# One pipeline of 33 steps for the later two thirds, its first weights fetched earlier, and the sums' steps spread wider

## The chip, the cores and the metric

The kernel runs on one core of one Trainium2 chip. The metric is device time in microseconds, the median of three runs: 2182.09 before (2181.76 to 2184.82). One core has five instruction streams, each executed in order: TensorE (PE, with its weight loads shown apart as PEld), VectorE (DVE), ScalarE (ACT), GpSimd (POOL) and SyncE (SP). In this kernel SP issues every DMA, so a DMA that waits on SP holds up all those written behind it. Engines and DMAs meet by semaphores only.

## The reference, cut to what matters

```python
q_p, k_p = phi(q_s), phi(k_s)                 # random-feature attention, 4 x 8 heads, 576 tokens, 128 features
x = (q_p @ (k_p.T @ v)) / (q_p @ z + 1e-6)    # -> x: 2304 tokens x 512
g = x @ w_gate                                # first layer, 512 -> 1536 -> 512
x = (silu(g) * (x @ w_val)) @ w_out
P = exp(x @ w_gate2 - max)                    # 2304 x 8, then 8 rounds of row and column scaling
for e in range(8):                            # second layer: every expert sees every token
    out += P[:, e:e + 1] * (np.maximum(x @ w1[e], 0) @ w2[e])     # 512 -> 1024 -> 512
```

All of it is in float32 to float32's accuracy. The kernel gets that from TensorE by splitting every operand into a high part (one copy by ACT that rounds) and a low part (a subtraction), and by three matmuls for each product: high x high, high x low, low x high.

## The kernel before

**The first layer** (`moe1`) has 6 groups of 256 hidden features, and for each group 6 blocks of 384 tokens. A block is two hidden units (`hunit`, 24 matmuls each) with the output unit of the block before between them (`ounit`, 24 matmuls, L753 to L755): 72 matmuls. Behind each hidden unit ACT runs the silu (L730), DVE multiplies (L731), ACT rounds the product to its high part (L734) and DVE makes the low part (L735); the output unit reads both. Between matmuls two generators are pumped, one step at a time: background tasks that prepare weights (`m1_task`, L155 on), and `sums` (L295), which prepares the combined forms of the second layer's down weights for later. `sums` has 32 rounds. A round loads one tile of weights (`raw2`), forms four combinations on POOL (L306 to L309), waits some steps, rounds two tiles on ACT (L322), subtracts on DVE (L324), and writes the results to DRAM (L317). A block of `moe1` has 14 places at which `sums` may take a step: five in each hidden unit, four in the output unit. So where an ACT instruction of `sums` stands against the silu of a hidden unit is set by counting steps.

**The second layer** multiplies by a scheme of seven products in place of eight 2x2 block products. For that the 768 tokens of a third need seven combined forms of x, each with high and low part: `b11`, `b21`, `b22`, `t1` to `t4`. `make_xops` builds them. A **quad** is the seven products for one group of hidden features.

The first third of the tokens (`moe2`) makes and uses the weights' forms and writes them to DRAM. For each of 16 groups m it runs `quad(m, 0)`, the output of group m-1 (`yunits`), `quad(m, 1)`. The outputs `yunits(15)` run alone at the end; `make_xops` for the second third is pumped beside them, and then the last weight forms are written.

The later two thirds (`thirds`) read finished weight forms from DRAM. For each third t there are 17 steps s. In a step, slots j = 0 to 13 each issue one product of the quads of group s (`quad_product`, 6 matmuls, L1237 to L1239) and one product of the outputs of group s-1 (`second_product`, 6 matmuls into half of a PSUM pair, L1321 to L1323); step 0 has only the former and step 16 only the latter. Behind every second output product DVE adds the pair to an accumulator (L1329). In step 16 DVE also combines the seven accumulators into four (L1332). Each quad is followed by gates (L1250, which need the token's gate weights `p`), ACT roundings (L1253), four subtractions on POOL (L1260), and low parts on DVE or POOL (L1257). Weights come as units of 512 KB into a ring of 11; `load` (L1189) asks for the next one or two at odd slots. `load_p` (L1203) fetches the gates' weights. The third's results are transposed by TensorE (`out_tile`, L1342), copied by ACT (L1344) and stored: those of the second third in step 0 of the last one, those of the last after everything.

Before the change the first units and the first gates' weights are asked for when the first third is over:

```python
1347  load(len(units))
1348  load_p(1, 0)
```

## Time and profile before

| what | value |
|---|---|
| median of three runs | 2182.09 us |
| the profiled execution, its own time | 2183.46 us |
| its span, first to last instruction | 2181.7 us |
| PE busy | 2106.2 us (97%) |
| DVE, POOL, ACT busy | 1340.2, 1014.1, 831.5 us (61, 46, 38%) |
| mean granted clock of TensorE | 0.986 of full speed |

What is not busy on PE is little, so the table alone says nothing of a change. The idle time lies in a few places: by the timeline, 22 us in the first layer, 19.5 us around 1189 to 1227 us where the first third ends, 6 us around 1670 to 1708 us where the second third ends, and some 6 us behind 2165 us. PE is also marked busy while it runs at half clock, which it does in some stretches behind such holes; the stage tables therefore carry the granted clock.

### The profile page before, as it was taken

To read this page: it belongs to the slowest core of one execution; us is meant where nothing else is said; L and a number is where in the kernel's file an instruction comes from. 1 tells how busy PE (TensorE), PEld (TensorE's weight loads), DVE (VectorE), ACT (ScalarE), POOL (GpSimd) and SP (SyncE) were. 2 spreads that over 40 slices of the span, in tenths; PEclk is the share of its full clock that TensorE was granted. 3 is DMA by queue.
4 is the path that set the end of the run, shared out by engine and by line. 5 is a ranking of instruction groups with operands and counts; after the bars stand their busy time and mean duration, and the time that the engine had idled before them with its cause. 6 is when DMAs were issued, how large, how long until landed. Compare 5 with 4: busy or idle time off the path is not lost.

```text
span 2181.7 us, 32894 instructions
## 1 busy us (share of the span) xinstructions
PE 2106.2 (97%) x12029; PEld 2025.7 (93%) x12029; DVE 1340.2 (61%) x2334; ACT 831.5 (38%) x1855; POOL 1014.1 (46%) x1034
## 2 busy tenths in 40 slices
PE   8999998998999999999998799999999999999998
PEld 7999998998999889989997799999998999999997
DVE  6886566666655654444445466666667666666666
ACT  6775333233244354334432332333233523332332
POOL 6663656565453444554551344344433443444442
PEclk9999999999999999999999899999999999999998
DMA  4332554554323567666674787777877777878773
GB/s 132 107 93 93 178 183 155 171 169 154 115 78 142 204 215 262 249 229 243 253 255 176 253 259 257 258 253 248 295 259 234 259 259 256 260 257 259 253 255 116
DMA packets 255153, 455.29 MB, mean 209 GB/s; under 512 B 42800, under 2 KB 137616, under 8 KB 250896
## 3 DMA queue, kind: packets, MB, share of 16 engines
q1 hardware_dynamic: 254992, 453.19, 62.3%
q8 instruction: 95, 1.56, 0.3%
q14 instruction: 66, 0.54, 0.1%
HBM read 327.76 MB, written 125.35 MB: 208 GB/s over the span
## 4 chain that ended last, share of the span: by engine, by line
PE 80%; DVE 6%; DMA 4%; POOL 4%; issue 3%; ACT 2%; SPq 1%; POOLq 0%; DVEq 0%; ACTq 0%
PE bank L1028 12%; PE pair L1321 7%; PE pair L1323 7%; PE pair L1322 7%; PE bank L1237 7%; PE bank L1239 7%; PE bank L1238 7%; PE bank L969 4%; PE bank L971 3%; PE bank L970 3%; DMA w2raw<-in_moe_w_dram 2%; PE bank L722 2%; PE bank L723 2%; PE bank L724 2%; PE bank L561 1%
## 5 line engine op out<-in xcount | busy, mean ns | idle before, releaser
L1237 PE MATMUL bank<-xh,ar 128*128 128x384 f32 x896 | 302.3, 337 | 20.3 <-DVE mt L1275 11.2
L1239 PE MATMUL bank<-xh,ar 128*128 128x384 f32 x896 | 301.1, 336 | 0.0
L1238 PE MATMUL bank<-xl,ar 128*128 128x384 f32 x896 | 301.1, 336 | 0.0
L1329 DVE TENSOR_TENSOR sums<-pair,sums 128x768 f32<-128x768 f32 x210 | 199.7, 951 | 48.3 <-PE pair L1323 48.0
L722 PE MATMUL bank<-xh,ar 128*128 128x384 f32 x576 | 192.8, 335 | 0.0
L724 PE MATMUL bank<-xh,ar 128*128 128x384 f32 x576 | 192.5, 334 | 0.0
L723 PE MATMUL bank<-xl,ar 128*128 128x384 f32 x576 | 192.4, 334 | 0.0
L1237 PEld LDWEIGHTS bank<-xh,ar 128*128 128x128 f32 x896 | 169.6, 189 | 22.3 <-DVE mt L1275 11.8
L1321 PE MATMUL pair<-xh,ar 128*128 128x384 f32 x538 | 180.6, 336 | 1.7 <-DVE sums L1329 1.7
L1322 PE MATMUL pair<-xl,ar 128*128 128x384 f32 x538 | 179.8, 334 | 0.0
L1323 PE MATMUL pair<-xh,ar 128*128 128x384 f32 x538 | 179.8, 334 | 0.0
L1238 PEld LDWEIGHTS bank<-xl,ar 128*128 128x128 f32 x896 | 169.5, 189 | 0.0
L1239 PEld LDWEIGHTS bank<-xh,ar 128*128 128x128 f32 x896 | 169.5, 189 | 0.0
L969 PE MATMUL bank<-xh,ar 128*128 128x384 f32 x448 | 151.7, 339 | 6.1 <-DVE st L1003 5.8
L237 POOL TENSOR_TENSOR ar<-w1raw,ar 128x512 fp32r<-128x512 f32 x64 | 65.3, 1030 | 193.4 <-ACT ar L235 92.6
L971 PE MATMUL bank<-xh,ar 128*128 128x384 f32 x448 | 150.8, 337 | 0.1
L970 PE MATMUL bank<-xl,ar 128*128 128x384 f32 x448 | 150.4, 336 | 0.0
L1044 DVE SCALAR_TENSOR_TENSOR ac<-bank,mt,ac 128x512 f32<-128x512 f32 x84 | 63.0, 750 | 127.8 <-PE bank L1028 126.0
L753 PE MATMUL bank<-ar,ar 128*128 128x384 f32 x288 | 101.7, 353 | 21.5 <-ACT ar L734 21.5
L1028 PE MATMUL bank<-ar,xh 128*128 128x512 f32 x402 | 115.2, 393 | 0.0
L324 DVE TENSOR_TENSOR ar<-w2raw,ar 128x512 fp32r<-128x512 f32 x64 | 58.9, 927 | 84.5 <-ACT ar L322 63.1
L722 PEld LDWEIGHTS bank<-xh,ar 128*128 128x128 f32 x576 | 108.1, 188 | 0.1
(270 smaller groups left out, 5662.3 us busy)
## 6 DMA issues: line engine op xcount, KB each, us to landing
ar<-w1forms SPq DMA_DIRECT2D x224, 512.0 KB, 4.9
ar<-w2forms SPq DMA_DIRECT2D x224, 512.0 KB, 4.5
w2forms<-ar SPq DMA_DIRECT2D x376, 128.0 KB, 3.5
w1forms<-ar SPq DMA_DIRECT2D x32, 1280.0 KB, 7.6
w2raw<-in_moe_w_dram SPq DMA_DIRECT2D x64, 512.0 KB, 3.9
w1raw<-in_moe_w_dram SPq DMA_DIRECT2D x32, 512.0 KB, 4.3
w1forms<-ar SPq DMA_DIRECT2D x32, 512.0 KB, 8.1
m1raw<-in_moe_w_gate_dram SPq DMA_DIRECT2D x12, 512.0 KB, 4.1
```

The lines of the kernel that those rows point to most:

```text
L722: nc.tensor.matmul(t, hi[:, c, fs], self.xh[:, c, cs], start=(c == 0), stop=False)
L723: nc.tensor.matmul(t, hi[:, c, fs], self.xl[:, c, cs], start=False, stop=False)
L724: nc.tensor.matmul(t, lo[:, c, fs], self.xh[:, c, cs], start=False, stop=(c == KC - 1))
L969: nc.tensor.matmul(g, ah[:, c, :], bh[:, c, :], start=(first and c == 0), stop=False, skip_group_check=not first)
L971: nc.tensor.matmul(g, al[:, c, :], bh[:, c, :], start=False, stop=(c == 1), skip_group_check=not first)
L1028: nc.tensor.matmul(y, a, w[:, fi % 2, ds], start=(first and x == 0 and k == 0 and fi == fis[0]), stop=(last and x == 1 and fi == fis[-1]))
L1237: nc.tensor.matmul(g, w[:, 0, d], bh[:, d, :], start=bool(first and d == 0), stop=False, skip_group_check=not first)
L1238: nc.tensor.matmul(g, w[:, 0, d], bl[:, d, :], start=False, stop=False, skip_group_check=not first)
L1239: nc.tensor.matmul(g, w[:, 1, d], bh[:, d, :], start=False, stop=(d == 1), skip_group_check=not first)
L1321: nc.tensor.matmul(pair[:, b, :], w[:, k, 0, ds], h, start=(k == 0), stop=False)
L1322: nc.tensor.matmul(pair[:, b, :], w[:, k, 0, ds], l, start=False, stop=False)
L1323: nc.tensor.matmul(pair[:, b, :], w[:, k, 1, ds], h, start=False, stop=(k == 1))
```

## The change

Five edits:

1. `sums` takes three more steps in each round: five in place of four between the combinations and the first rounding, one before the next load and one behind it.
2. The ring of units, the first six loads and the list of what to load become methods. `load_units(6)` stands ahead of the last quad of the first third, and five more together with the first gates' weights ahead of `yunits(15)`. The remaining writes of weight forms stand there too. So on SP these loads come ahead of the six stores of the first third's results.
3. `make_forms` takes the place of `make_xops(..., True)`. Forms come in the order in which the quad uses them, and seven of their eleven subtractions of 128x768 move from DVE to POOL.
4. The later two thirds are one loop of 33 steps: step 16 runs the first quads of the last third beside the last outputs of the second. The forms of the last third are made from slot 8 of step 15 to slot 1 of step 16. The second third's results are transposed in slots 0 to 5 of step 17, through one PSUM bank.
5. The last step takes its outputs in another order (`LAST2`), with the sums of accumulators spread over it and one of them, (5, 7), on POOL, in both thirds. The last six tiles go through six different PSUM banks and six buffers, copied by ACT and DVE in turn.

```diff
+    LAST2 = (1, 3, 5, 6, 7, 2, 4)
@@ sums
-            for _ in range(4):
+            for _ in range(5):
                 yield
@@
                     for _ in range(3):
                         yield
+            yield
             if i + 1 < len(order):
                 t = load(i + 1)
+            yield
             for c in range(one, 2):
                 write(c)
@@ new
+    def make_forms(self, pf, qf):
...
+        p0, p1, q0, q1 = pf[:, 0:2, :], pf[:, 2:4, :], qf[:, 0:2, :], qf[:, 2:4, :]
+
+        def form(n, src, eng):
+            h, l = [self.xslot(x, *self.XS[n]) for x in range(2)]
+            nc.scalar.copy(h, src)
+            eng.tensor_tensor(l, src, f(h), op=ALU.subtract)
+
+        def sub(dst, a, b):
+            g.tensor_tensor(dst, a, b, op=ALU.subtract)
+
+        form("b11", p0, g)
+        yield
+        sub(p0, q0, p0)
+        yield
+        form("t1", p0, v)
+        sub(q0, q1, q0)
+        yield
+        sub(p0, q1, p0)
+        yield
+        form("t2", p0, v)
+        form("b21", p1, g)
+        yield
+        sub(p1, p1, p0)
+        form("t3", q0, v)
+        yield
+        form("b22", q1, g)
+        yield
+        form("t4", p1, v)
+        yield
@@ moe2
+            if m == NG2 - 1:
+                self.set_units()
+                self.load_units(6)
             hs = hs + drive(quad(m, 1), self.PACE['g2'], self.PACE['r01'] if m == 0 else self.PACE['rq'])
@@
-        xg = self.make_xops(*stage, True)
+        for i in range(2):
+            self.need(("w2", NG2 - 1, i))
+        self.set_weights()
+        self.load_units(5)
+        while self.writes:
+            self.writes.popleft()()
+        xg = self.make_forms(*stage)
         self.bg.appendleft(xg)
         drive(yunits(*pend))
         for _ in xg:
             pass
-        while self.writes:
-            self.writes.popleft()()
@@ thirds, second_product
             if m == NG2 - 1:
-                for d, a in {2: [(2, 1)], 5: [(3, 5)], 6: [(1, 6), (7, 1), (3, 1), (5, 7)], 4: [(4, 7)]}.get(n, ()):
-                    v.tensor_tensor(acc[d], acc[d], acc[a], op=ALU.add)
+                rest = [(7, 1), (4, 7), (5, 7)]
+                sums = {1: [(2, 1)], 5: [(3, 5)], 6: [(1, 6), (3, 1)]}
+                sums.setdefault(7 if step > m else 6, []).extend(rest)
+                for d, a in sums.get(n, ()):
+                    eng = nc.gpsimd if d == 5 else v
+                    eng.tensor_tensor(acc[d], acc[d], acc[a], op=ALU.add)
@@ thirds, the loop
+        for g in range(self.STEPS):
+            if g == NG2 - 1:
+                xg = self.make_forms(*stage)
+            for j in range(14):
+                if g < 2 * NG2:
+                    quad_product(g, j)
+                run_later()
+                if g == NG2 + 1 and j < 6:
+                    out_tile(1, j, self.banks[3 if self.nquad % 2 else 0], spare((6, 7)[j % 2]), nc.scalar)
+                if g:
+                    second_product(g - 1, j)
+                if 14 * g + j >= 14 * (NG2 - 1) + 8 and g <= NG2:
+                    next(xg, None)
+                if j % 2:
+                    self.load_units((g < 2 * NG2) + (g > 0))
+                if j == 11 and g % 2 == 0 and g < 2 * NG2 - 2:
+                    self.load_p(g // 2 + 1)
+                now[0] += 1
...
+        room = [spare(n) for n in (1, 6, 7)] + [x[:, 0:DM] for x in self.lasts]
+        banks = self.banks[0:4] + [self.pairs[1][:, i * 512:(i + 1) * 512] for i in range(2)]
         for i in range(6):
-            out_tile(2, i)
+            out_tile(2, i, banks[i], room[i], (nc.scalar, v)[i % 2])
```

What this does to the order of instructions, at three places. First ACT in the third group of the first layer, where `w2raw` is a tile of `sums` (its rounding is L322 before and L323 after), `mt <- bank` is a silu and `m1raw` and `cv` belong to the weight tasks. Before:

```order
L734 CAST ar_62<-mt_2394 128x384
L322 CAST ar_62<-w2raw_0_4029 128x512 x2
L730 ACTIVATE mt_2394<-bank_71 128x384
L734 CAST ar_62<-mt_2394 128x384
L199 CAST ar_61<-cv 128x512
L182 ACTIVATE m1raw_1_0_4056<-m1raw_1_0_4056 128x512
L322 CAST ar_62<-w2raw_1_4130 128x512
L730 ACTIVATE mt_2394<-bank_69 128x384
L734 CAST ar_62<-mt_2394 128x384
L322 CAST ar_62<-w2raw_1_4130 128x512
L730 ACTIVATE mt_2394<-bank_71 128x384
```

And after, further into the layer:

```order
L323 CAST ar_62<-w2raw_0_4591 128x512 x2
L733 ACTIVATE mt_2394<-bank_69 128x384
L737 CAST ar_62<-mt_2394 128x384
L733 ACTIVATE mt_2394<-bank_71 128x384
L737 CAST ar_62<-mt_2394 128x384
L200 CAST ar_61<-cv 128x512
L183 ACTIVATE m1raw_1_0_4672<-m1raw_1_0_4672 128x512
L323 CAST ar_62<-w2raw_1_4711 128x512 x2
L733 ACTIVATE mt_2394<-bank_69 128x384
L737 CAST ar_62<-mt_2394 128x384
L733 ACTIVATE mt_2394<-bank_71 128x384
L737 CAST ar_62<-mt_2394 128x384
```

The roundings of `sums` still stand ahead of silus, but a round comes every 15 steps in place of 12, with five steps between its combinations and its first rounding.

Second, SP where the first third ends: `w1forms` and `w2forms` are the weight forms in DRAM (a row `w2forms<-...` writes them, a row `ar<-...` loads a unit), `pweights` the gates' weights, `out_dram` the results. Before:

```order
L1382 DMA out_dram<-ac_6623 128x512 x2
L1382 DMA out_dram<-ac_6622 128x512 x4
L287 DMA w2forms<-w2a 128x256 x3
L287 DMA w2forms<-w2b 128x256 x3
L1199 DMA ar_61<-w1forms 128x2x512 x2
L1199 DMA ar_61<-w1forms 128x1024
L1199 DMA ar_61<-w1forms 128x2x512 x3
L1199 DMA ar_62<-w1forms 128x2x512 x2
L1196 DMA ar_62<-w2forms 128x1024
L1199 DMA ar_62<-w1forms 128x2x512
L1196 DMA ar_62<-w2forms 128x1024
L1205 DMA last_10643<-pweights 128x6x128
```

After:

```order
L1222 DMA ar_61<-w1forms 128x2x512 x2
L1222 DMA ar_61<-w1forms 128x1024
L1222 DMA ar_61<-w1forms 128x2x512 x3
L1232 DMA last_10531<-pweights 128x6x128
L1222 DMA ar_62<-w1forms 128x2x512 x2
L1219 DMA ar_62<-w2forms 128x1024
L1222 DMA ar_62<-w1forms 128x2x512
L1219 DMA ar_62<-w2forms 128x1024
L288 DMA w2forms<-w2a 128x256 x3
L288 DMA w2forms<-w2b 128x256 x3
L1438 DMA out_dram<-ac_6623 128x512 x2
L1438 DMA out_dram<-ac_6622 128x512 x4
```

All eleven loads and the gates' weights stand ahead of the six stores, and six loads and the gates' weights ahead of anything that the last outputs release.

Third, POOL where the second third ends, with `xl` the low parts and `st`, `mt`, `last`, `sums` the working tiles. Before (two quads of the last steps of the second third):

```order
L1260 TENSOR_TENSOR sums_10639<-sums_10639,sums_10641 128x384
L1257 TENSOR_TENSOR xl<-last_10645,xh 128x384 x2
L1260 TENSOR_TENSOR mt_2394<-mt_2394,last_10645 128x384
L1260 TENSOR_TENSOR mt_2394<-last_10645,mt_2394 128x384
L1260 TENSOR_TENSOR st_6625<-last_10645,mt_2394 128x384
L1260 TENSOR_TENSOR mt_2394<-mt_2394,st_6625 128x384
```

After, between the same two quads (L875 and L878 are `make_forms`):

```order
L1313 TENSOR_TENSOR sums_10654<-sums_10654,sums_10656 128x384
L875 TENSOR_TENSOR xl<-st_6625,xh 128x2x384
L878 TENSOR_TENSOR st_6625<-mt_2394,st_6625 128x768
L878 TENSOR_TENSOR mt_2394<-mt_2394 128x768
L878 TENSOR_TENSOR st_6625<-mt_2394,st_6625 128x768
L1310 TENSOR_TENSOR xl<-last_10533,xh 128x384
L875 TENSOR_TENSOR xl<-st_6625,xh 128x2x384
L1310 TENSOR_TENSOR xl<-last_10533,xh 128x384
L878 TENSOR_TENSOR st_6625<-st_6625 128x768
L1313 TENSOR_TENSOR mt_2394<-mt_2394,last_10533 128x384
L1313 TENSOR_TENSOR mt_2394<-last_10533,mt_2394 128x384
L1313 TENSOR_TENSOR st_6625<-last_10533,mt_2394 128x384
```

Seven wide subtractions of the forms (the seventh stands a row below) now stand among the narrow ones of the last quad of the second third.

## Rows read from the trace of the kernel before

**Rows 1.** The page: busy time of each engine, share of span, instructions.
```profile
PE 2106.2 (97%) x12029; PEld 2025.7 (93%) x12029; DVE 1340.2 (61%) x2334; ACT 831.5 (38%) x1855; POOL 1014.1 (46%) x1034
```

**Rows 2.** Windows, first layer's six groups: length, busy PE PEld DVE ACT POOL, clock.
```profile
178.10:255.56 77.46, 75.71 (x471) 74.71 (x470) 42.94 (x73) 34.17 (x71) 34.07 (x34) 1.00 0.44 140
255.56:340.90 85.34, 79.39 (x434) 77.85 (x433) 52.20 (x89) 27.83 (x55) 50.66 (x50) 0.96 0.54 172
340.90:426.14 85.24, 78.68 (x433) 76.90 (x433) 52.41 (x92) 26.60 (x51) 49.91 (x47) 0.96 0.53 170
426.14:510.89 84.75, 79.06 (x433) 77.41 (x433) 53.38 (x93) 26.34 (x52) 49.94 (x48) 0.96 0.52 168
510.89:589.02 78.13, 76.22 (x433) 74.69 (x433) 48.53 (x88) 23.77 (x46) 41.27 (x36) 1.00 0.42 136
589.02:673.00 83.98, 83.98 (x486) 82.87 (x486) 46.60 (x83) 32.58 (x68) 32.20 (x25) 1.00 0.22 80
```

**Rows 3.** Windows, two blocks of the fourth group.
```profile
466.70:479.18 12.48, 12.48 (x73) 12.48 (x73) 6.28 (x13) 4.14 (x8) 6.45 (x7) 1.00 0.55 171
491.66:510.89 19.23, 15.57 (x73) 15.16 (x73) 11.62 (x23) 4.81 (x10) 10.77 (x12) 0.82 0.51 170
```

**Rows 4.** Waits, 178 to 589: total us, times, longest.
```profile
ACT ar L322 <- POOL w2raw L308: 97.4, 22, 7.3
POOL w2raw L306 <- DMA w2raw<-in_moe_w_dram: 91.6, 25, 20.8
...
ACT ar L199 <- POOL cv L196: 34.7, 14, 4.0
...
ACT ar L322 <- DMA w2forms<-ar: 26.2, 9, 4.0
...
PE bank L753 <- ACT ar L734: 21.5, 11, 4.0
```

**Rows 5.** One combination of the sums (L308), and landing of their loads (L273).
```profile
L308 POOL TENSOR_TENSOR w2raw<-w2raw 128x256 f32<-128x256 f32 x32 | 26.0, 813 | 2.5
...
DMA to landing us min/median/max: 3.7/3.9/6.9
```

**Rows 6.** Windows: first seam, second seam, one full step, tail.
```profile
1188.90:1229.30 40.40, 20.71 (x91) 19.79 (x92) 12.48 (x20) 6.99 (x15) 8.70 (x8) 0.75 0.75 262
1668.78:1710.31 41.53, 35.13 (x199) 32.56 (x199) 39.35 (x50) 17.66 (x33) 12.00 (x11) 1.00 0.68 210
1710.31:1739.40 29.09, 29.09 (x169) 28.99 (x168) 16.25 (x24) 14.36 (x27) 15.37 (x16) 1.00 0.81 280
2166.00:2181.70 15.70, 6.17 (x24) 4.57 (x24) 4.46 (x5) 3.52 (x6) 0.00 (x0) 0.58 0.32 100
```

**Rows 7.** Timeline of PE, first seam: start, us, ... idle before and its releaser.
```profile
1196.71 0.66 PE L1237 MATMUL bank<-xh,ar 128*128 128x384 f32 x1 [7.84 <-DMA ar<-w1forms]
...
1216.74 0.69 PE L1237 MATMUL bank<-xh,ar 128*128 128x384 f32 x1 [10.80 <-DVE mt L1275]
```

**Rows 8.** Timeline in yunits(15): the first addition, and PE's fifth output.
```profile
1179.39 0.75 DVE L1044 SCALAR_TENSOR_TENSOR ac<-bank,mt,ac 128x512 f32<-128x512 f32 x1
...
1183.27 0.39 PE L1028 MATMUL bank<-ar,xh 128*128 128x512 f32 x1
```

**Rows 9.** Subtractions of 128x768 by engine: ns min/median/max.
```profile
L835 POOL TENSOR_TENSOR mt<-mt,mt x3: 2046/2150/2166, 626.0 to 632.3; 128x768 f32<-128x768 f32 x3
...
L832 DVE TENSOR_TENSOR xl<-st,xh x8: 946/949/959, 1173.8 to 1688.4; 128x768 fp32r<-128x768 f32 x8
L832 POOL TENSOR_TENSOR xl<-mt,xh x4: 1842/1848/1852, 640.0 to 664.9; 128x768 fp32r<-128x768 f32 x4
```

**Rows 10.** Low parts on DVE (two SBUF inputs): ns min/median/max.
```profile
L1257 DVE TENSOR_TENSOR ar<-last,ar x25: 549/559/1406, 1251.3 to 2143.9; 128x384 fp32r<-128x384 f32 x25
```

**Rows 11.** Timeline of the tail: PE, ACT, SP.
```profile
2169.55 0.69 PE L1342 MATMUL pair<-ident,sums 128*128 128x128 f32 x2 [3.55 <-DVE sums L1329]
...
2177.99 0.59 ACT L1344 COPY sums<-pair 128x512 f32<-128x512 f32 x1 [1.25 <-PE pair L1342]
...
2175.80 3.13 SPq L1382 DMA_DIRECT2D out_dram<-sums  x3
```

More of the change, by code (lines that the diff above doesn't have):

```diff
@@ L1140, in spread, with flat, order2, set_units @@
         nc.sync.dma_start(self.pd, self.mb[0:n, :])
+    def flat(self, j):
+        return 7 * (j // 7) + self.PLACE[self.USE[j % 7]]
+    def order2(self, step):
+        return self.LAST2 if step == 2 * NG2 - 1 else self.USE2
+    STEPS = 2 * NG2 + 1
+    def set_units(self):
+        def cut(t, o, n):
+            return [t[:, o + i * 1024:o + (i + 1) * 1024] for i in range(n)]
+        self.units = cut(self.ar1, 6144, 3) + cut(self.ar1, 0, 3) + cut(self.ar2, 0, 5)
+        self.todo, self.where, self.nunit = deque(), {}, 0
+        for g in range(self.STEPS):
+            for u in range(7):
+                for which, i in (("w1", g), ("w2", g - 1)):
+                    if 0 <= i < 2 * NG2:
+                        self.todo.append((which, i, u))
+    def load_units(self, n):
+        nc = self.nc
+        for _ in range(min(n, len(self.todo))):
+            key = self.todo.popleft()
+            which, i, u = key
+            m = i % NG2
+            d = self.where[key] = self.units[self.nunit % len(self.units)]
+            self.nunit += 1
+            if which == "w2":
+                k = self.USE2.index(self.order2(i)[u])
+                nc.sync.dma_start(f(d), self.w2f[:, m, k].rearrange("p k x d -> p (k x d)"))
+            else:
+                a, b = sorted((self.flat(2 * u), self.flat(2 * u + 1)))
+                nc.sync.dma_start(f(d).rearrange("p (n c) -> p n c", n=2), self.w1f[:, m, a:b + 1:b - a, :])
+    def set_weights(self):
+        self.lasts = [self.raw.tile([P, 1024], F32, tag=f"raw{i}", name=f"last{i}") for i in range(3)]
+        self.pb = [r[:, 0:768] for r in self.lasts[0:2]]
+        self.load_p(0)
+    def load_p(self, n):
+        t, e = divmod(n, E)
+        src = self.pd.rearrange("(t e) c -> e t c", e=E)[e, 6 * t:6 * t + 6, :]
+        self.nc.sync.dma_start(self.pb[e % 2].rearrange("p (t c) -> p t c", c=P), src.partition_broadcast(P))
     def thirds(self, xs, t3, t4):
         nc, af, v = self.nc, self.af, self.nc.vector
-        ar1, ar2, USE, USE2 = self.ar1, self.ar2, self.USE, self.USE2
+        ar1, USE, where, pb = self.ar1, self.USE, self.where, self.pb
         def cut(t, o, n, w):
             return [t[:, o + i * w:o + (i + 1) * w] for i in range(n)]
-        units = cut(ar1, 6144, 3, 1024) + cut(ar1, 0, 3, 1024) + cut(ar2, 0, 5, 1024)
         pieces = []
@@ L1342, in out_tile @@
                 nc.tensor.transpose(tr[:, d * P:(d + 1) * P], a[:, d % 2, cs], self.ident)
-            o = acc[(1, 6, 7)[i % 3]].rearrange("p b t -> p (b t)")[:, 0:DM]
-            nc.scalar.copy(o, tr)
+            if eng is v:
+                v.tensor_copy(o, tr)
+            else:
+                nc.scalar.copy(o, tr)
             self.store(6 * t + tt, o, slice(0, DM))
-        load(len(units))
-        load_p(1, 0)
-        for t in (1, 2):
-            for s in range(NG2 + 1):
-                if s == NG2 and t == 1:
-                    xg = self.make_xops(*stage, True)
-                for j in range(14):
-                    if s < NG2:
-                        quad_product(t, s, j)
-                    run_later()
-                    if s:
-                        second_product(t, s - 1, j)
-                    if s == NG2 and t == 1:
-                        next(xg, None)
-                    if s == 0 and t == 2 and j % 2 and j > 1:
-                        out_tile(1, j // 2 - 1)
-                    if j % 2:
-                        load((s < NG2) + (s > 0))
-                    if j == 11 and s % 2 == 0 and s < NG2:
-                        e = s // 2 + 1
-                        if e < E or t == 1:
-                            load_p(t + e // E, e % E)
-                    now[0] += 1
-                if t == 1 and s == 10:
-                    self.fetch(stage, 2)
-            if t == 1:
-                for _ in xg:
-                    pass
@@ new lines, in spare @@
+        def spare(n):
+            return acc[n].rearrange("p b t -> p (b t)")[:, 0:DM]
+        for g in range(self.STEPS):
+            if g == NG2 - 1:
[15 more added lines that the diff above has]
+                now[0] += 1
+            if g == 10:
+                self.fetch(stage, 2)
```

51 lines of the change are left out of this document (12 added, 39 removed).

## The prediction

> **What bounds the kernel now.** I read the page first: PE is busy 97% of the span [rows 1], so only its holes and its half-clock stretches can be won. Then the stage windows, to see in which stage PE is less busy than the stage is long; then the waits of the stage, for what ended last; then the timeline of each seam. There are four places.
>
> The first layer. A block of 72 matmuls that nothing disturbs takes 12.48 us, all of it busy; a block of the same 73 rows takes 19.23 us where it is disturbed, and the clock falls to 0.82 there [rows 3]. Six undisturbed blocks are 74.9 us. Groups two to five take 85.34, 85.24, 84.75 and 78.13 us, so they lose 10.4, 10.3, 9.9 and 3.2; the first group idles 77.46 - 75.71 = 1.8; the sixth, where `sums` is over, idles nothing [rows 2]. Together 35.6 us: 22 of them idle, the rest half clock behind the holes. PE's wait is always for ACT's rounding L734 (21.5 us) [rows 4]. That instruction isn't slow, it is late: ACT stood before at a rounding of `sums` that waited for POOL's third combination (97.4 us), or for DRAM writes (26.2), or at a weight task's rounding (34.7), and POOL itself stood 91.6 us for the load of `sums` [rows 4].
>
> The first seam. From the end of the first third to the first output product of the second third it is 40.40 us, at clock 0.75 [rows 6]. One hole of 7.84 us waits for the first unit; one of 10.80 waits, through a gate on DVE, for the first gates' weights [rows 7].
>
> The second seam. The end of the second third and step 0 of the last take 41.53 us; a full step of 28 products takes 29.09, or 1.04 each [rows 6]. Between the same two points lie 29 products, 30.2 us, and 24 transposes at 0.11, 2.6 us. So 8.7 us are lost.
>
> The tail. From the last output product to the end it is 15.70 us [rows 6]; PE stands 3.55 us for the last sums on DVE [rows 11].
>
> **The change, part by part**, against the profiled execution's own 2183.46 us (1.8 us more than its span).
>
> *Sums spread.* A round hangs together by events: its last low part frees the tile, the next load lands 3.9 us later, three combinations take 3 x 0.81 = 2.4, and only then can the first rounding run: 6.3 us [rows 5]. By steps, that rounding stood 9 steps behind the low part, and now stands 12. A block has 14 steps in 12.48 us, so 0.89 each: 8.0 us before, 10.7 after. Before, 1.7 us of margin were left, which any late DVE or POOL instruction used up; after, 4.4. So the waits on L308 should go, and those on the writes of the round before with them. What stays is the third kind, 34.7 of 34.7 + 97.4 + 26.2, or 22%: 7.8 of the 35.6 us. New is the length: 32 rounds of 15 steps are 480 of the some 500 steps, where 384 were enough, so four rounds fall into the sixth group, in a mode with one slot, which never ran before: the second rounding waits for the write of the first. I bound its cost by nothing and by the whole 4.0 us that one such wait took at most [rows 4], so 0 to 16 us; I take 3, since in three of the four rounds no silu that PE soon needs stands behind it. Gain 35.6 - 7.8 - 3 = 24.8. Bounds: 0 (all waits stay) and 35.6.
>
> *First seam.* On SP six units and the gates' weights now stand ahead of everything that the last outputs release, so both holes go. Without them step 0 needs 15 x 1.04 = 15.6 us, and 40.4 - 15.6 = 24.8 can be won. What is late next is `make_forms`. In DVE's order three low parts of the forms stand ahead of the first output addition of `yunits(15)`, and the third waits by way of ACT for POOL: from 1173.8, four wide instructions of 1.85 to 2.15 us [rows 9] end at about 1181.9; two more ACT roundings and two low parts of 0.95 bring the addition to 1185.2, where it stood at 1179.39 [rows 8]. PE's fifth output, at 1183.27 [rows 8], needs the bank that this addition frees, so PE stands until about 1186.1: 2.9 us. Such a hole was followed by half clock elsewhere (a disturbed block of rows 3), so I add 1.7; and 1 us because step 0 asks each quad of DVE and POOL in half the usual time. Gain 24.8 - 5.6 = 19.2; bounds 14 (the forms twice as late) and 24.8.
>
> *Second seam.* The merged steps hide what made up the 8.7 us, but load POOL: seven wide instructions, 14 us [rows 9], in eight slots of 2.08 = 16.6 us, beside POOL's usual 15.37 in 29.09 [rows 6], or 8.8 us. POOL comes out some 6 us late, ACT waits for its subtractions in order, and ACT's copies out of PSUM behind them come late for the quads of step 16: about 4 us of PE. In step 17 the sum (5, 7), 2.1 us, stands on POOL ahead of low parts, and all six tiles pass one bank by ACT: 3 us more. Gain 8.7 - 7 = 1.7; bounds -8 (waits twice as long, plus step 17's) and 8.7.
>
> *Tail.* Behind the last product only one addition of 0.95 is left, and (5, 7) on POOL ends about 1 us behind it. 24 transposes at 0.11 to 0.21 us, two engines for the copies of 0.59, no shared bank; then SP, with issues of 0.34 for whole tiles and 0.6 for the halves, is the longest, about 6.2 us after the last product, and 2.8 us for the last landing and the end, as in before (from the last issue's end, 2178.93, to 2181.7) [rows 11]. 9.5 in place of 15.7: gain 6.2; bounds 4 and 8.
>
> Sum: 24.8 + 19.2 + 1.7 + 6.2 = 51.9, so 2131.6 us; the profiled execution is 1.4 above the median of the runs, so 2130.
>
> **A rule against it.** A low part on DVE, with two inputs in SBUF, takes 0.55 us but up to 1.41 [rows 10], and the long ones lie beside a POOL instruction. The Trainium skill (SBUF — State Buffer, "Who interferes with whom") says why: such a DVE instruction and a POOL one that reads SBUF exclude each other for the whole instruction. The trace agrees in kind. By that rule the wide POOL instructions, twice as long, hold DVE twice as long as any row here shows, and moving work from DVE to POOL relieves nothing while both are wanted. This is the second rival.
>
> **Rivals.**
> - The sums keep ACT. What speaks for it: over a third of ACT's waits were not for the combinations [rows 4], roundings still stand ahead of silus, and the one-slot mode is untried. Against it: the margin of 4.4 us. Only 8 us of the layer come back: 2147.
> - The second seam backs up. In eight slots DVE has 16.25 x 16.6 / 29.09 = 9.3 us of its own [rows 6], four wide low parts (3.8), and 12 instructions with two SBUF inputs that may each take 0.86 more [rows 10], 10.3: 23.4 in 16.6. PE then waits 7 us in step 16, as much again behind it and 3 in step 17, 17 in place of 7: 2140. Against it: the usual beside-POOL instruction is only half as late.
> - The loads don't come early, because SP stands at a wait for PE ahead of them. Then the first seam stays: 2149. Against it: in front of them stand only writes whose data are made by then.
> - More is won than I count: all of the layer but 3 us, nearly all of the first seam, 6 us at the second, 7 in the tail: 33 + 24 + 6 + 7 = 70, so 2112.
> - Slower: ACT in the first layer. Before, PE waited 11 times [rows 4], so the 35.6 us are 3.2 for each time that a round of `sums` stood badly; with 12 steps against 14 a round meets a block in only seven positions. With 15 steps all 14 occur. If each of the 32 rounds then costs 3.2 us, the layer loses 102 us in place of 35.6, and with 27.1 us won elsewhere the kernel takes 2222. It decides from 62.7 / 32 = 2.0 us a round; before it was 1.1. Against it: the wait itself should be gone.
>
> **Chances.** Forecast 0.56 (2120 to 2140 by itself), sums keep ACT 0.15, second seam 0.12, more won 0.09, loads late 0.03, slower 0.04. A measurement of this kernel tells about 0.2%, 4 us, from no change; all cases but the last are faster by more than that, and 0.01 is left for several of these at once that end even: faster 0.95, same 0.01, slower 0.04. The range must reach to most of the two larger rivals and of the better case: 2112 to 2149.
>
> **What would show it.** In the first layer's windows five groups of 75 to 78 us and a sixth near 86, and ACT's wait at the sums' rounding for POOL near nothing; a wait for the w2forms writes in the sixth group if the one-slot mode costs. At the first seam no idle on a unit or on the gates' weights, one hole of about 3 us inside `yunits(15)`, and 16 to 17 us from the third's end to the first output product. At the second, POOL full for some 20 us and several PE holes of 1 to 2 us on ACT's copies, in steps 16 and 17. In the tail 9 to 10 us behind the last product. I am wrong in the main term if the layer's groups still take 80 us or more, and in the second if PE idles for a unit or for the gates' weights there.

## The result, and the profile after

The changed kernel takes 2154.3 us (median of 4 runs, 2153.0 to 2156.1); the kernel before took 2182.6 beside it. The ratio is 0.9869, 95% interval 0.9852 to 0.9886: 28 us faster, where 52 were forecast, and 5 us outside the range. The profiled execution spans 2151.2 us in place of 2181.7. (One of the four executions of e11 below ran at a mean granted clock of 0.85, took 2288.6 us and is left out there.) Between the same instructions in the two traces the 30.5 us come out so (us won, minus is lost):

| stretch | forecast | measured | from |
|---|---|---|---|
| ahead of the first layer | 0 | -1.0 | 178.10, now 179.06 |
| first layer, six groups | 24.8 | 14.1 | 494.9, now 480.8 |
| first third, with the hole in `yunits(15)` | -4.6 | -4.0 | 515.9, now 519.9 |
| its end to the first output product | 23.8 | 22.3 | 40.4, now 18.1 |
| second seam | 1.7 | -6.1 | 157.7, now 163.8 |
| tail, from the last product's end | 6.2 | 5.3 | 15.9, now 10.6 |

(The forecast's first seam, 19.2, is the third and the fourth row together.) Two rows are far off, the first layer and the second seam. First the page of the changed kernel, to set against [rows 1]; it tells nothing of the two: the shares hardly moved, and of the busy times only POOL's rose.

```profile
PE 2093.4 (97%) x12029; PEld 2015.7 (94%) x12029; DVE 1335.3 (62%) x2321; ACT 830.0 (39%) x1852; POOL 1041.4 (48%) x1050
```

The windows of the layer's six groups after the change, as [rows 2]:

```profile
179.06:254.54 75.48, 75.48 (x471) 74.69 (x470) 36.77 (x71) 33.75 (x70) 29.48 (x30) 1.00 0.41 131
254.54:331.89 77.35, 75.98 (x434) 74.72 (x434) 45.10 (x83) 27.00 (x53) 42.99 (x43) 1.00 0.47 146
331.89:411.71 79.82, 75.94 (x434) 74.72 (x434) 52.56 (x94) 24.81 (x47) 47.79 (x44) 1.00 0.51 159
411.71:487.13 75.42, 75.41 (x433) 74.79 (x433) 45.20 (x86) 24.56 (x47) 38.56 (x37) 1.00 0.48 147
487.13:567.26 80.13, 76.84 (x434) 76.15 (x433) 54.61 (x89) 25.46 (x48) 44.22 (x42) 0.98 0.49 158
567.26:659.86 92.60, 86.89 (x486) 84.24 (x486) 60.92 (x97) 36.46 (x76) 49.32 (x42) 0.98 0.46 150
```

Groups two to five were to be 75 to 78 us and two of them are 80; the sixth, 83.98 before, is 8.6 longer. The waits of the first five groups, as [rows 4]:

```profile
ACT ar L200 <- POOL cv L197: 59.6, 18, 8.0
...
POOL w2raw L307 <- DMA w2raw<-in_moe_w_dram: 32.9, 12, 8.0
...
ACT ar L323 <- POOL w2raw L309: 31.0, 13, 4.7
...
ACT ar L323 <- DMA w2forms<-ar: 22.0, 9, 4.2
...
PE bank L756 <- ACT ar L737: 7.6, 4, 3.0
```

ACT's wait for the sums' third combination fell from 97.4 us to 31.0, where almost nothing was forecast; its wait at the rounding of a weight task rose from 34.7 to 59.6. The timeline shows what that is in the third group, whose second block begins at 344.37 (start, us, ... idle before and its releaser; three engines, then PE):

```profile
342.71 0.43 DVE L185 TENSOR_SCALAR cv<-m1raw 128x512 int32<-128x512 int32 x1 [4.23 <-POOL ar L202]
...
348.71 1.28 POOL L197 TENSOR_TENSOR cv<-cv,m1raw 128x512 f32<-128x512 f32 x1
...
350.02 0.62 ACT L200 CAST ar<-cv 128x512 fp32r<-128x512 f32 x1 [7.95 <-POOL cv L197]
...
350.55 0.48 ACT L733 ACTIVATE mt<-bank 128x384 f32<-128x384 f32 x1
```
```profile
352.22 0.44 PE L756 MATMUL bank<-ar,ar 128*128 128x384 f32 x1 [3.01 <-ACT ar L737]
```

Six tasks of 11 steps are 66; the pumps of six blocks give 60. What is left of the last task the line `self.flush()` in the next group's first block issues at once: its chain on DVE and POOL, then its rounding on ACT, all ahead of the silu (L733) of that first block's second hidden unit. ACT waits 7.95 us for the chain to end, the silu comes late, and PE stands 3.01 us at the output unit that reads it, which is issued in the second block. By blocks most of the loss lies there: the second blocks of groups two to five take 14.06, 16.01, 13.03 and 17.73, where 12.48 would do, 10.9 us in all; all other blocks of the first five groups together lose 2.9. In the kernel before, these second blocks lost 11.4 (17.17, 15.07, 14.61, 14.43), and the sixth blocks of groups one to four 20.8, among them the disturbed one of [rows 3]. What ACT stood at tells the two apart: ahead of PE's hole in the sixth block of groups two, three and four it waited 7.25 us at a rounding of `sums`, as in this row of the kernel before (PE then stood 4.01 us). Ahead of PE's holes in the second blocks it waited last at L199, 3.3 to 4.0 us, and earlier for `sums` too.

```profile
413.68 0.62 ACT L322 CAST ar<-w2raw 128x512 fp32r<-128x512 f32 x1 [7.25 <-POOL w2raw L308]
```

The losses of the sixth blocks are gone.

In the sixth group PE's longest hole reads so:

```profile
617.62 4.22 POOL L838 TENSOR_TENSOR mt<-mt,mt 128x768 f32<-128x768 f32 x2
...
617.88 2.31 DVE L252 TENSOR_TENSOR ar<-w1raw,ar 128x512 fp32r<-128x512 f32 x1
...
620.11 2.28 DVE L325 TENSOR_TENSOR ar<-w2raw,ar 128x512 fp32r<-128x512 f32 x1
...
622.31 0.17 DVE L945 TENSOR_TENSOR mt<-bank,mt 128x24 f32<-128x24 f32 x1
```
```profile
622.54 0.44 PE L756 MATMUL bank<-ar,ar 128*128 128x384 f32 x1 [3.87 <-DVE mt L945]
```

Beside POOL's wide subtractions (L838) two low parts of DVE take 2.3 us each, where 0.69 is usual. One of them, L325, belongs to `sums` and is new in this group; L945, for which PE waits, stands behind both. By blocks, the group's excess of 8.6 us is 5.7 in this fourth block (20.14, before 14.41) and 2.5 in the second (16.39, before 13.90).

The seams and the tail, as [rows 6] (windows: first seam, second seam from output product 196 to 266, tail), and under it the same stretch of the second seam before:

```profile
1179.75:1197.89 18.14, 16.05 (x91) 15.40 (x90) 12.82 (x20) 7.21 (x15) 8.77 (x8) 1.00 0.64 199
1609.25:1773.08 163.83, 152.64 (x864) 149.26 (x864) 109.11 (x158) 58.97 (x120) 80.92 (x69) 0.99 0.76 242
2140.63:2151.20 10.57, 3.22 (x25) 2.50 (x23) 3.55 (x5) 1.76 (x3) 1.42 (x1) 0.93 0.48 149
```
```profile
1640.59:1798.29 157.70, 151.29 (x864) 147.76 (x865) 112.67 (x166) 59.48 (x120) 63.74 (x61) 1.00 0.76 251
```

At the first seam PE waits neither for a unit nor for the gates' weights. The hole that was forecast inside `yunits(15)` came:

```profile
1172.41 0.50 PE L1064 MATMUL bank<-ar,xh 128*128 128x512 f32 x1 [3.89 <-DVE ac L1080]
```

In the second seam POOL is busy 17 us more. Its timeline, engine by engine, where PE first stands:

```profile
1632.42 2.20 DVE L1310 TENSOR_TENSOR ar<-sums,ar 128x384 fp32r<-128x384 f32 x1
...
1635.99 1.82 DVE L1303 SCALAR_TENSOR_TENSOR last<-last,last 128x384 f32<-128x384 f32 x1
```
```profile
1643.92 2.16 POOL L878 TENSOR_TENSOR st<-st 128x768 f32<-128x768 f32 x1
1646.05 1.01 POOL L1313 TENSOR_TENSOR mt<-mt,last 128x384 f32<-128x384 f32 x1
```
```profile
1647.09 0.51 ACT L1306 CAST xh<-mt 128x384 fp32r<-128x384 f32 x1 [5.47 <-POOL mt L1313]
```
```profile
1641.99 0.45 PE L1375 MATMUL pair<-ar,ar 128*128 128x384 f32 x1 [2.57 <-DVE sums L1383]
1651.15 0.45 PE L1290 MATMUL bank<-xh,ar 128*128 128x384 f32 x1 [1.58 <-ACT sums L1323]
1657.42 0.45 PE L1290 MATMUL bank<-xh,ar 128*128 128x384 f32 x1 [1.83 <-DVE sums L1328]
```

The quads' own low part and gate, 0.55 us elsewhere, take 2.20 and 1.82; POOL reaches the quad's subtractions (L1313) only behind the forms' (L878); ACT waits 5.47 us for them. Both engines are late, and PE stands three times for more than 1.5 us. In step 17 it stands again, at the first output tile:

```profile
1679.22 0.44 PE L1399 MATMUL bank<-ident,sums 128*128 128x128 f32 x2 [2.27 <-DVE sums L1303]
```

### The profile page after: what moved, and what is told of

Its sections match the earlier page's. It is cut to its first block, busy times and chain, and to the rows that moved or that the text cites. A ratio compares the mean times of both kernels' runs of the same rounds, so it can differ in the third digit from the quotient of the medians.

```text
span 2151.2 us, 32864 instructions
## 1 busy us (share of the span) xinstructions
PE 2093.4 (97%) x12029; PEld 2015.7 (94%) x12029; DVE 1335.3 (62%) x2321; ACT 830.0 (39%) x1852; POOL 1041.4 (48%) x1050
## 4 chain that ended last, share of the span: by engine, by line
PE 76%; DVE 3%; issue 3%; POOL 2%; ACT 1%; DMA 1%; SPq 0%; POOLq 0%; DVEq 0%; ACTq 0%
PE bank L1064 11%; PE pair L1375 7%; PE bank L1290 7%; PE bank L1292 7%; PE bank L1291 7%; PE pair L1377 7%; PE pair L1376 7%; PE bank L1005 3%; PE bank L1007 3%; PE bank L1006 3%; PE bank L726 3%; PE bank L727 3%; PE bank L725 3%; PE bank L756 1%; PE bank L758 1%
## 5 line engine op out<-in xcount | busy, mean ns | idle before, releaser
L1291 PEld LDWEIGHTS bank<-xl,ar 128*128 128x128 f32 x896 | 168.4, 188 | 0.0
L726 PEld LDWEIGHTS bank<-xl,ar 128*128 128x128 f32 x576 | 108.6, 189 | 0.0
```

Source lines behind the costliest of these rows:

```text
L726: nc.tensor.matmul(t, hi[:, c, fs], self.xl[:, c, cs], start=False, stop=False)
L1291: nc.tensor.matmul(g, w[:, 0, d], bl[:, d, :], start=False, stop=False, skip_group_check=not first)
```

## The experiments

Each is the changed kernel with the edit shown, timed beside the kernel before; the times are medians of 4 executions (e11: 3). The windows come from one profiled execution each, so the spread of a window over kernels that leave its stage alone is given where a difference is small.

**e1, the sums' steps undone.**

```
-            for _ in range(5):
+            for _ in range(4):
...
-            yield
             if i + 1 < len(order):
                 t = load(i + 1)
-            yield
```

> The changed kernel with the steps of sums as before the change (12 steps a round: the fifth step ahead of the first rounding and the two new ones around the load are taken out), all else as changed. Theory: the whole gain of the first layer comes from these three steps, so the layer gives back what it gained: its end, 691.3 us in the changed kernel, goes back to about 704 us, and the time from 2154.3 to about 2167. Rival: the layer's gain has partly another source (weights' loads or the state of the clock); then the end stays below 699 and the time below 2162.

2167.3 us (ratio 0.9938, 0.9923 to 0.9953), 13.0 more; the first quad of the third begins 11.8 us later, from a layer that starts 2.1 earlier. The sixth blocks lose again, while the second blocks go on losing as before. The two windows are a second and a sixth block of the fourth group:

```profile
437.13:451.74 14.61, 13.02 (x73) 12.41 (x73) 9.14 (x16) 4.13 (x8) 8.96 (x8) 1.00 0.50 160
490.16:509.60 19.44, 15.61 (x73) 15.20 (x73) 11.85 (x24) 4.87 (x10) 10.81 (x12) 0.82 0.52 164
```

So the layer's gain is the sums' steps, and it is the sixth blocks; the sixth group, too, is back at 84.0.

**e2, no steps left for the flush.**

```
-            self.pump(self.PACE['h'])
+            self.pump(self.PACE['h'] + fi)
```

> The changed kernel with one pump step more behind the second hidden unit of each block, so that the six weight tasks of a group (66 steps) are through when the group is (60 steps before), and the flush in the next group's first block finds nothing left. Theory: the two holes of 3.0 us at 352 and 507 us stand where the flush issues the last six steps of a weight task at once, its rounding on ACT ahead of a silu; they and the half clock behind one go, ACT's wait at the weight rounding falls from 67.6 us to under 40, and the layer ends 6 to 9 us earlier, time about 2147. Rival: the weight rounding is late because POOL and DVE are held by the combinations and low parts of sums, wherever the flush stands; then holes of the same size come up at other blocks and the time is 2152 to 2158.

2142.9 us (0.9825, 0.9810 to 0.9839), 11.4 less, more than expected. The second block of the fifth group, after the change and in e2:

```profile
499.61:517.34 17.73, 14.44 (x74) 13.75 (x73) 12.56 (x21) 5.04 (x10) 10.22 (x10) 0.90 0.35 119
```
```profile
494.53:507.01 12.48, 12.48 (x73) 12.48 (x73) 9.89 (x16) 4.83 (x10) 7.93 (x8) 1.00 0.55 169
```

All second blocks of groups two to five take 12.48 now. The five groups gain 8.4 us (388.2 to 379.8): the 10.9 of the second blocks, less some 2.5 that now come up in other blocks, which is the rival in part; the sixth group gains 2.0. One number went against the expectation: ACT's wait at the weight rounding was to fall below 40 us; in the first five groups it doubled, from 59.6 to

```profile
ACT ar L200 <- POOL cv L197: 122.3, 28, 7.5
```

PE's own wait for ACT there is 2.5 us in all, after 7.6. The sum of a wait on ACT is no measure of what PE loses by it.

**e3, a form's low part behind the first output addition.**

```
-                    yield 1 + len(ys) // 3
+                    yield 1
```

> The changed kernel with one step of the forms, not two, pumped behind the fourth output of the first third's last outputs: the third low part of the forms (t2 on DVE) then stands behind the first output addition. Theory: that low part, which waits by way of ACT for POOL, is what holds the first output addition and with it PE for 3.9 us at 1172; the hole shrinks to under 1 us, the half clock behind it goes, and the time falls by 4 to 5.5 us to about 2149.5. Rival: the later steps of the forms come as much later, so that the second third's first products wait for them: the hole moves to 1180 to 1190 and the time stays at 2154.

2147.7 us (0.9846, 0.9831 to 0.9860), 6.6 less. The last 30 us of the first third, after the change and in e3:

```profile
1149.75:1179.75 30.00, 26.11 (x118) 22.34 (x117) 14.10 (x17) 8.88 (x14) 13.43 (x7) 0.94 0.79 269
```
```profile
1145.12:1175.12 30.00, 30.00 (x143) 26.07 (x142) 13.14 (x17) 8.51 (x14) 12.22 (x7) 1.00 0.92 315
```

The hole and the half clock behind it are gone, the third, from its first quad product to the start of its last output, is 5.7 us shorter (513.8 in place of 519.5; the nine other kernels that leave this stretch alone took 519.8 to 522.3), and the seam behind it as long as before, 18.5. The cause forecast for this hole is shown.

**e4, the sums of accumulators spread at the second seam.** The last step of the second third in the order `LAST2`:

```
-        return self.LAST2 if step == 2 * NG2 - 1 else self.USE2
+        return self.LAST2 if step % NG2 == NG2 - 1 else self.USE2
...
-                sums.setdefault(7 if step > m else 6, []).extend(rest)
+                sums.setdefault(7, []).extend(rest)
```

> The changed kernel with the last step of the second third also in the order of its last step (LAST2), which spreads the sums of accumulators over slots 7 to 9 of that step in place of five in a row in its last three slots. Theory: the first output tile's transposes wait 2.27 us at 1679 because five additions of 0.96 us stand on DVE ahead of the gate that reads their bank; spread, the hole goes, and with it 2 to 4 us of the second seam: about 2151. Rival: DVE is as full in slots 7 to 9 (behind the forms' low parts), so the additions delay the quads there, and the seam loses as much as it wins: 2153 to 2157.

2153.1 us (0.9867, 0.9850 to 0.9883). In this order one product reads a form whose buffer has been filled anew, so this kernel computes something else; the amount of work is the same. The wait of the first tile fell from 2.27 us to

```profile
1681.14 0.66 PE L1399 MATMUL bank<-ident,sums 128*128 128x128 f32 x4 [0.23 <-DVE sums L1303]
```

and the seam from 163.8 to 161.7. The mechanism holds for the hole; what it is worth isn't told: the time is 1.2 us less, and the five other kernels that leave this seam alone took 162.1 to 163.4 for it.

**e5, no forms at the second seam.**

```
-                    next(xg, None)
+                    pass
```

> The changed kernel without the operand forms at the second seam: the seven forms of the last third and their four subtractions are left out, so the last third multiplies the operands of the second third again; products, sums, output tiles and loads stay. It gives the price of the forms where they stand now. Theory: the forms on POOL and their low parts on DVE make the subtractions and gates of the quads late in step 16; without them the holes at 1636 to 1658 us and the half clock behind them go, 6 to 8 us, and only the hole of 2.3 at the first output tile stays: the seam from output product 196 to 266 takes about 156.5 in place of 163.8, the time about 2147. Rival: the merged steps themselves (a full step of 28 products, with sums and tiles on top) are late there; then the seam stays above 161 and the time above 2151.

2145.5 us (0.9835, 0.9821 to 0.9850). The window from product 196 to 266:

```profile
1611.67:1765.54 153.87, 151.38 (x865) 149.36 (x865) 99.36 (x154) 53.90 (x113) 64.65 (x62) 0.99 0.81 257
```

This kernel computes something else too; it leaves the forms out. All holes of step 16 are gone; the one at the first tile stays, 2.27 us as before. The forms cost 10.0 us where they stand; what is left over the undisturbed seam, 157.7 - 8.7 = 149.0, is 4.9 for step 17. (The time fell by 8.9 only: in the profiled execution the first third took 2.7 us longer than in the changed kernel's.)

**e6 and e10, the forms' work moved from POOL to DVE**, at the second seam alone: the three low parts (b11, b21 and b22 alike), and in e10 also the four subtractions (the second pair of lines). The lines are shortened: in the kernels the engine is an argument that only the second seam's call sets.

```
-        form("b11", p0, g)
+        form("b11", p0, v)
...
-            g.tensor_tensor(dst, a, b, op=ALU.subtract)
+            v.tensor_tensor(dst, a, b, op=ALU.subtract)
```

> The changed kernel with the three low parts b11, b21 and b22 of the second seam's forms on DVE in place of POOL. Theory A: POOL's queue is what is late (ACT stood 5.5 us at a rounding for POOL's subtractions); POOL is rid of 6.3 us, DVE gets 2.9, the seam of 163.8 gets 3 to 5 shorter, time about 2150. Theory B: DVE is the full engine there, its instructions 1.2 to 2.2 us instead of 0.55 to 0.95 beside POOL's wide ones; then three more on DVE cost as much as POOL's relief gives, seam 163 to 167, time 2153 to 2157.

> The changed kernel with all the wide work of the second seam's forms on DVE: the three low parts as in e6 (seam 160.9) and the four subtractions as well. The forms cost 10 us where they stand (e5). Theory A, POOL's wide instructions hold both POOL's queue and, beside them, DVE: without them DVE's instructions fall back to 0.55 and 0.95, the four subtractions cost it 3.8, and the seam falls to 156 to 159, time about 2148. Theory B, DVE's own work is the limit of these eight slots: 11 wide instructions are 10.5 us on top of some 9, in 16.6, so DVE is 3 us late and the quads wait as much again: seam 162 to 166, time 2153 to 2157.

2152.9 (0.9867, 0.9852 to 0.9882) and 2153.5 (0.9868, 0.9854 to 0.9883). The windows, e6 and then e10:

```profile
1612.52:1773.46 160.94, 152.85 (x865) 150.31 (x865) 111.13 (x161) 58.94 (x120) 74.39 (x66) 0.98 0.78 246
```
```profile
1611.88:1774.42 162.54, 153.44 (x865) 150.92 (x865) 111.55 (x165) 59.15 (x120) 66.77 (x62) 0.98 0.76 243
```

The low parts win 2.9 us (e11 and e12, which have the same edit, took 159.6 and 160.8): POOL's queue was late, theory A of e6. The subtractions win nothing, against theory A of e10: the window is 1.6 longer than e6's in this one execution, which is within the spread of such windows. One hole of PE that waits for an addition on DVE has grown, from 2.57 us to 3.80 in e6 and 4.56 in e10, and of the others in step 16 only one of 0.52 is left, in e10:

```profile
1645.82 0.69 PE L1375 MATMUL pair<-ar,ar 128*128 128x384 f32 x1 [3.80 <-DVE sums L1383]
```
```profile
1646.65 0.45 PE L1375 MATMUL pair<-ar,ar 128*128 128x384 f32 x1 [4.56 <-DVE sums L1383]
```

In the 18.65 us up to the end of that hole DVE is busy 17.97 us in e10: with POOL relieved, DVE is full (theory B). Wherever the 11 wide instructions stand, most of the 10 us stay.

**e7, sums that end ahead of the sixth group**: e2, and rounds of 13 steps.

```
-            yield
             if i + 1 < len(order):
                 t = load(i + 1)
-            yield
```

> The kernel with 11 pump steps a block (e2, 2142.9 us) and rounds of sums of 13 steps: the fifth step ahead of the first rounding stays, the two around the load are taken out, so 32 rounds are 416 steps and end before the sixth group (420). Theory: sums in the sixth group (low parts on DVE beside the wide POOL instructions of the operand forms, writes with one slot) cost about 7 us there, and go; a round's margin over the 6.3 us of its chain falls from 4.4 to 2.6 us, which still is enough: the layer ends 5 to 7 us earlier, time about 2137. Rival: at 13 steps the first rounding of sums holds ACT again at some blocks, as with 12: then holes of 1 to 3 us come back in groups one to five and the time is 2143 or more.

2161.1 us (0.9907, 0.9892 to 0.9922): the rival's time, and worse. The sixth group wins most of what was forecast: its blocks take 83.8 us after 90.64 in the changed kernel and 88.60 in e2, and its second and fourth block, 13.89 and 14.41, are as in the kernel before. But groups one to five take 402.1 us in place of e2's 379.8; PE stands in all five. The rival's reason is not what the trace shows: of the ten holes of 0.5 us or more, all come behind a wait of ACT at the weight task's rounding (L200, 2.6 to 7.6 us), and only two of them also behind one of 1.7 us at a rounding of `sums`. Why the weight tasks are late with rounds of 13 steps was not taken apart.

```profile
580.05:663.82 83.77, 82.83 (x474) 80.79 (x474) 50.64 (x82) 32.90 (x69) 32.68 (x26) 1.00 0.24 84
```

**e8, the output tiles one slot later**, in slots 1 to 5 of step 17.

```
-                if g == NG2 + 1 and j < 6:
+                for i in [(), (0,), (1,), (2,), (3,), (4, 5)][j] if g == NG2 + 1 and j < 6 else ():
```

> The changed kernel with the six output tiles of the second third one slot later in step 17 (slots 1 to 5, the last two in one slot). Theory: the first tile's transposes wait 2.3 us for a gate on DVE that reads their bank; a slot later (2.1 us) they find it read, the hole goes and the seam gets about 2 us shorter, time 2152. Rival: PE would stand a moment later anyway, at the pair that DVE's addition behind that gate frees, or at the two tiles of one slot, whose bank waits for ACT's copy: no gain, 2154 to 2155.

2156.3 us (0.9883, 0.9867 to 0.9900), the seam 165.8: the rival. PE stands 3.14 us at the pair of the first output product instead, for the DVE addition behind the same gate. What holds PE there is DVE, not the tile's place; that the five additions are what makes DVE late is e4's.

**e9, the first third's operand forms on DVE.**

```
-        v = nc.vector if direct else nc.gpsimd
+        v = nc.vector
```

> The changed kernel with the four subtractions and four low parts of the first third's operand forms, 768 wide, which POOL works out in blocks 2 to 4 of the sixth group, on DVE. Theory: the sixth group loses 8.5 to 9 us because low parts on DVE (1.68, 2.31 and 2.28 us, where 0.56 to 0.68 is usual) run only between or beside POOL's wide instructions, and the fourth round's low part of sums, new in that block, comes on top; with the wide work on DVE (0.95 each) nothing holds it, the hole of 3.9 us at 622 goes with the half clock behind it, and the time falls by 4 to 6 us to about 2149. Rival: DVE is simply full in these blocks with the four rounds of sums; eight more instructions of 0.95 make it later, the group's blocks 2 to 4 get 2 to 6 us longer, time 2156 to 2160.

2151.6 us (0.9862, 0.9848 to 0.9877). The time is 2.7 us under the changed kernel's, less than forecast, and the intervals overlap. The blocks tell more: the sixth group's fourth block takes 16.10 us in place of 20.14 (17.83 to 20.17 in the six other kernels that leave the group alone), its hole 1.39 in place of 3.87. The same low part there:

```profile
619.63 0.68 DVE L325 TENSOR_TENSOR ar<-w2raw,ar 128x512 fp32r<-128x512 f32 x1
```

**e11 and e12, the edits that won together**: e2, e3 and e6; and with e9's as well.

> The changed kernel with three edits that each won by itself: 11 pump steps a block (e2, 11.4 us), one step of the forms behind the fourth output (e3, 6.6), the second seam's low parts on DVE (e6, seam 2.9 shorter). They lie in different stages, so theory: they add up to 17 to 21 us, time 2133 to 2137. Rival: part of what e3 and e6 showed was the length of half-clock stretches, which come out at 3.4 or 6.8 us from execution to execution, and the sum is 3 to 5 us less: 2138 to 2141.

> The three edits of e11 (2134.1 us) and the fourth of e9, the first third's operand forms on DVE. Theory: in e11 the sixth group still loses about 7 us (blocks 2 to 4 of 16.2, 15.6 and 14.7 where 14.4 would do); with the wide work on DVE blocks 2 and 3 lose 1 to 3 us less, and the time falls to 2130 to 2133. Rival: with 11 steps a block the weights' units of the next layer stand elsewhere in these blocks, DVE is full with them, and nothing is won: 2134 to 2136.

2133.5 us (0.9779, 0.9760 to 0.9799) and 2132.8 (0.9774, 0.9758 to 0.9790): 21 us under the changed kernel and 48 under the one before. The gains of e2 (11.4), e3 (6.6) and e6 (2.9 of its seam) add up. The fourth edit is no gain beside e2 that the intervals tell: the fourth block of the sixth group is 2.5 us longer than in e11, the third 1.6 shorter. (With e2's extra step alone the fourth block takes 15.57: the low part L252 no longer stands beside the subtractions there.)

## Why the prediction was wrong

**Sums spread (24.8, measured 14.1).** The mechanism was right for what it named: with the round's margin up, the sixth blocks' 20.8 us came back (e1), though a third of ACT's wait for the third combination stayed, at no cost to PE that shows. The step that failed is "the third kind, 34.7 of 34.7 + 97.4 + 26.2, or 22%: 7.8 of the 35.6 us". It took ACT's idle time by releaser for shares of what PE lost. What PE loses to the third kind is the flush's, 11.4 us before and 10.9 after, not 7.8 (e2 takes all of the 10.9 away). Of the 10.7 us that the layer fell short, 5.1 lie in the first five groups, there and in small losses elsewhere that stayed, and 5.6 in the sixth. The windows of the blocks of the kernel before hold both losses apart, one in the second blocks of groups two to five and one in the sixth of groups one to four; I had shown one such block and not asked where it stood. (That both recur by the group fits their steps: a group's 84 are seven rounds of 12, and the flush comes once in it.)

**The sixth group (3, measured 8.6).** The place was right, the cause not. I priced the wait for the write in the one-slot mode; the largest part, 4.0 us in the fourth block (e9; one kernel without that edit had 2.3 of them by itself), is DVE's low parts beside POOL's wide subtractions. In e7, without rounds in the group, the second and fourth blocks, 8.2 of the 8.6 us, are as before. How the rest of the 8.6 is shared between the one slot, the low parts and the weight tasks was not taken apart. The price could have been read: in the kernel before one low part stood beside the same subtractions and took 2.33 us, at no cost to PE (that block took 14.41); with a second one behind it, PE stands. The two rows of the kernel before:

```profile
630.40 2.33 DVE L251 TENSOR_TENSOR ar<-w1raw,ar 128x512 fp32r<-128x512 f32 x1
...
630.14 4.29 POOL L835 TENSOR_TENSOR mt<-mt,mt 128x768 f32<-128x768 f32 x2
```

**First seam (19.2, measured 18.3).** Right in both holes that went, in the new one and its cause (e3). The hole was 3.89 us for 2.9, 5.6 with its half clock (the rest of the third lost 1.6 less than before), and step 0 kept 2.5 for 1. That the sum comes so near is in part luck of the profiled execution: in the other kernels with this hole the third took up to 522.3 us in place of 519.5, and with that the seam's gain is 15.5.

**Second seam (1.7, measured -6.1).** The places and the engines were right, the size not: step 16 costs 10.0 us (e5) where I took 4, step 17 4.9 where I took 3. The step that failed is "POOL comes out some 6 us late [...] about 4 us of PE": it counts POOL's queue as the one delay. DVE's two-input instructions beside POOL I left to the rival, and set that aside because "the usual beside-POOL instruction is only half as late". Both delays are there: e6 relieves POOL and wins 2.9, and then PE waits for DVE (e6, e10). Whether less wide work in these eight slots, the forms spread over more of them, would win was not tried.

**Tail (6.2, measured 5.3).** Right; PE stands 1.09 us at the first transposes for (5, 7) on POOL, as forecast:

```profile
2142.10 0.66 PE L1399 MATMUL bank<-ident,sums 128*128 128x128 f32 x4 [1.09 <-POOL sums L1390]
```

Of the rivals, the second seam's (17 us lost in place of 7) came nearest there, 14.9. The first, that the sums keep ACT, did not come as such: the layer fell short by the flush and the sixth group. I had given a chance to each shortfall alone, and two came at once. With these two stages at their measured size the sum is 33 in place of 52 and the forecast 2148.5, just inside the range. Small terms carried the result out of it: about 1 us each in the first seam, the tail and ahead of the first layer, and some 3 because the profiled execution, which the forecast took to be 1.4 us above the median, was 1.3 below it after the change.

**The rule.** On DVE's gates after the change (ns, least, median, most), a gate that reads a bank of PSUM and one SBUF operand never took longer than 558, one with both inputs in SBUF up to 1825:

```profile
L1303 DVE SCALAR_TENSOR_TENSOR last<-last,last x42: 557/558/1825, 1194.2 to 2090.9; 128x384 f32<-128x384 f32 x42
...
L1303 DVE SCALAR_TENSOR_TENSOR last<-bank,last x21: 542/557/558, 1210.6 to 2109.4; 128x384 f32<-128x384 f32 x21
```

The Trainium skill (SBUF — State Buffer, "Who interferes with whom") says that a DVE instruction with two SBUF inputs contends with a POOL one that reads SBUF, and that one with at most one SBUF input, outside the modes that use both ports, does not. The traces agree, in this split, and in e9, where the low part falls from 2.28 to 0.68 once POOL's work beside it is gone.

## What to carry over

Find lost time by the blocks of the engine that bounds the kernel, against an undisturbed block, and by where in the loop the long blocks stand; the idle sums of other engines do not divide that loss, and may double while the time falls. A background task whose steps don't divide evenly over its loop leaves a remainder that can come out in one lump: here one step more in each block took it away. When several stages can each fall short, add the shortfalls in the range.

## What the runs showed of the hardware

Beside POOL instructions of 1.8 to 2.2 us back to back, a two-input DVE instruction ran to 2.3 us (usually 0.69) and 2.2 (usually 0.55): about as long as POOL's own, so DVE fell to POOL's pace. [Rows 10] had shown no more than 1.41; the 2.33 at L251 stood in the trace before, in another stage. And the same hole of 3.89 us in `yunits(15)` cost differently from execution to execution by the half clock beside it: the third took 519.5 us in the changed kernel and 522.2 in e5, with the same instructions there and a mean granted clock over its last 30 us of 0.94 and 0.89.
